# The count of the remaining experts, loaded into all engines' registers two blocks before the end of the work instead of after it

## The chip, the cores and the metric

One core of a Trainium2 chip. The metric is the device time of one execution in microseconds (us); the kernel before was timed three times. The engines are named as in the profile: PE (matmuls) and PEld (its weight loads), DVE, ACT, POOL and SP; a "q" behind a name (PEldq, SPq) marks what the engine's sequencer does by itself: waits for semaphores, register loads, branches.

## What is computed

Three layers follow each other. The change lies in the last one, a mixture of experts in which each token takes one expert, and may keep that of the token before it:

```python
def _moe2_ref(x, w_gate, w_local, w1, w2) -> np.ndarray:
    ...
    for b in range(B):
        prev_e = -1
        for s in range(S):
            fresh_e = int(np.argmax(logits[b, s]))
            if s == 0 or local_gate[b, s] < 0.5:
                e = fresh_e
            else:
                e = prev_e if prev_e >= 0 else fresh_e
            prev_e = e
            ...
            h = np.maximum(x[b, s] @ w1[e], 0.0)
            out[b, s] = p[e] * (h @ w2[e])
```

There are 4 batch rows of 576 tokens, a width of 512, 8 experts and 1024 hidden units an expert. Ahead of it stand a linear attention (4 x 8 heads) and a mixing and feed-forward layer (512 to 2048 to 512).

## The kernel before

Activations lie transposed in `y`, features on partitions and tokens along the row. Each float32 product is made of three matmuls: weights and activations are split into a high part and a rest (`hi`, `lo`, `hhi`, `hlo`, `w[:, 0]`, `w[:, 1]`), and high times high, high times rest and rest times high are summed in PSUM.

The instruction order is that in which the Python code issues them (`manual_schedule`); each engine runs its own instructions in that order, and semaphores hold it where it needs another engine's result. The feed-forward layer and the experts are worked through in `blocks`, `n` of them. A block is one group of weights (a unit: four pieces for the first matrix, four for the second) against a stretch of 384 or 288 tokens. For each batch row `b` the kernel first finds out, on the chip, which expert most tokens use (`route(b)`), and runs this one expert for all 576 tokens: two units of weights (`g` 0 and 1), each against two stretches (`c` 0 and 1) of 288 tokens. So the last block, `n - 1`, is row 3, g 1, c 1, and `n - 2` is row 3, g 1, c 0.

`mm1(i, f)` is the first matrix of block `i`, hidden rows `f` (12 matmuls), followed by ACT's ReLU into `hhi` (L511) and DVE's rest `hlo` (L512). `mm2(i, d)` is the second matrix (12 matmuls), and for g 1 it is followed by DVE's addition into `y` (L534), a product with the tokens' probabilities (L537; POOL's, but DVE's for the last two pieces of the last block), and the store of the piece (L548). `work()` orders them: while block `i` is worked on, the ReLU pieces of block `i + 1` are made ahead, so an iteration `i` issues `mm1(i+1, 0)`, then `mm2(i, 0..3)`, then `mm1(i+1, 1..3)`. Between these pieces `side(i, step)` issues what runs beside them, among it `w_prep`, which splits the next piece of weights: a cast on ACT (L168) and a subtraction on DVE (L172).

Tokens may use other experts than the one that was run. `route` writes into `flags`, 32 numbers on one partition, a one for each other (row, expert) that is in use. Behind the last block DVE sums them (L815), casts the sum to an integer (L816), and `values_load` (L817) has each of the five engines load it into a register (TENSOR_LOAD). A loop (L819) then runs once per such expert. In this execution no pass of the loop was run: each engine tests its register, branches past the loop's code, and meets the others in the closing barrier.

Of the kernel before, what the change touches and what calls it, by code (L numbers as in the profile page):

```python
# [7 lines left out]
F32 = mybir.dt.float32  # L8
F32R = mybir.dt.float32r
U32 = mybir.dt.uint32  # L10
I32 = mybir.dt.int32
ACTF = mybir.ActivationFunctionType
ALU = mybir.AluOpType
AX = mybir.AxisListType.X
# [22 lines left out]
def model(ctx, tc, kq, vx, wphi, ident, up, vp, wff, wg, wmoe, rconst, outT):  # L37
    nc = tc.nc
# [137 lines left out]
    late = {}  # L176
# [24 lines left out]
    def w_ahead():  # L201

        if at["dma"] < len(pieces) and at["dma"] < at["prep"] + 2 and (
                pieces[at["dma"]][0].kind == "ffn" or pieces[at["dma"]][0].b in pidx):
            w_dma()
# [261 lines left out]
    ul = {0: later}  # L467
# [29 lines left out]
    def mm1(i, f):  # L497
        u, hf, t0, n_, _ = blocks[i]
        w = need(u, f)
        hi, lo = ul[hf]  # L500
        sl = slice(t0, t0 + n_)
        ps = fps()[:, :n_]
        for k in range(4):
            wh = w[:, 0, k * 128:(k + 1) * 128]
            wl = w[:, 1, k * 128:(k + 1) * 128]
            nc.tensor.matmul(ps, lhsT=wh, rhs=hi[:, k, sl], start=(k == 0), stop=False)  # L506
            nc.tensor.matmul(ps, lhsT=wh, rhs=lo[:, k, sl], start=False, stop=False)  # L507
            nc.tensor.matmul(ps, lhsT=wl, rhs=hi[:, k, sl], start=False, stop=(k == 3))  # L508
        hhi = h_p.tile([128, CF], F32R, tag="hhi", name="hhi")[:, :n_]
        hlo = h_p.tile([128, CF], F32R, tag="hlo", name="hlo")[:, :n_]  # L510
        nc.scalar.activation(out=hhi, in_=ps, func=ACTF.Relu)  # L511
        nc.vector.scalar_tensor_tensor(out=hlo, in0=ps, scalar=0.0, in1=f32(hhi), op0=ALU.max, op1=ALU.subtract)  # L512
        hh[i, f] = (hhi, hlo)
        if last[u] == i:
            used.add((units.index(u), f))

    def mm2(i, d):
        u, hf, t0, n_, c = blocks[i]
        ps = fps()[:, :n_]
        for f in range(4):  # L520
            hhi, hlo = hh[i, f]
            w = need(u, 4 + f)
            wh = w[:, 0, d * 128:(d + 1) * 128]
            wl = w[:, 1, d * 128:(d + 1) * 128]
            nc.tensor.matmul(ps, lhsT=wh, rhs=hhi, start=(f == 0), stop=False)  # L525
            nc.tensor.matmul(ps, lhsT=wl, rhs=hhi, start=False, stop=False)  # L526
            nc.tensor.matmul(ps, lhsT=wh, rhs=hlo, start=False, stop=(f == 3))  # L527
        if last[u] == i and d == 3:
            used.update((units.index(u), 4 + f) for f in range(4))
        dst = y[:, hf, d, t0:t0 + n_]  # L530
        if u.kind == "moe" and u.g == 0:
            nc.scalar.copy(out=dst, in_=ps)
            return
        nc.vector.tensor_tensor(out=dst, in0=ps, in1=dst, op=ALU.add)  # L534
        if u.kind == "moe":
            eng = nc.vector if i + 1 == n and d > 1 else nc.gpsimd
            eng.tensor_tensor(out=dst, in0=dst, in1=scale[u.b][:, c * CH:(c + 1) * CH], op=ALU.mult)  # L537
            outs.append((outT[d * 128:(d + 1) * 128, 2 * S * hf + t0:2 * S * hf + t0 + n_], dst))
            if i + 1 == n:
                store(0)  # L540
# [3 lines left out]
    def store(keep):  # L544
        while len(outs) > keep:
            dst, src = outs.pop(0)
            eng = nc.scalar if keep else nc.sync
            eng.dma_start(out=dst, in_=src)  # L548
# [138 lines left out]
    def drain(lst):  # L687
        while lst:
            if next(lst[0], "end") == "end":
                lst.pop(0)  # L690


    n = len(blocks)
    splits = []

    def side(i, step):

        u, _, _, _, c = blocks[i]
        if u.kind == "ffn":
            if splits and step in (2, 6):  # L700
                split_rows(*splits.pop(0))
            if u.g < 3:
                for _ in range(2 if step in (3, 7) else 1):
                    if not preps and room() and at["prep"] < min(8 * u.g + 16, 8 * u.g + 10 + 4 * c // 3 if u.g else 16):
                        preps.append(w_prep())
                    prep_step()
                if late:
                    w_ahead()
            else:
                if step == 0 and c in (2, 3, 5):  # L710
                    bg.append(route({2: 0, 3: 1, 5: 2}[c]))
                bg_step()
                if 0 not in pidx:
                    bg_step()
                if 0 in pidx and step % 2:
                    if at["prep"] < 8 * len(ffn_units) + 8 and room():
                        preps.append(w_prep())
                        drain(preps)
                        w_ahead()
        else:  # L720
            k = units.index(u)
            if u.b == 0 and u.g == 0 and c == 0 and step == 0:
                bg.append(route(3))
            bg_step()
            if c == 0 and step == 4 and u.g == 0:
                bg.insert(0, scale_row(u.b))
            if k + 1 < len(units) and at["prep"] < min(8 * (k + 2), 8 * k + 8 + 4 * c + (step + 1) // 2) and room():
                v = units[k + 1]
                if v.b not in pidx:
                    drain(bg)  # L730
                preps.append(w_prep())
                drain(preps)
                w_ahead()

    def work():

        for f in range(4):
            mm1(0, f)
            yield
        for i in range(n):  # L740
            u = blocks[i][0]
            if u.kind == "moe" and u.g == 1 and u.b not in scale:
                drain(bg)
            if i + 1 < n:
                mm1(i + 1, 0)
            side(i, 0)
            yield
            for d in range(4):
                mm2(i, d)
                side(i, 1 + d)  # L750
                yield
            if i + 1 < n:
                for f in range(1, 4):
                    mm1(i + 1, f)
                    if f > 1:
                        store(1)
                    side(i, 4 + f)
                    yield

    todo = work()  # L760
    ahead = [0]

# [27 lines left out]
    ul_p = late["ul"] = ctx.enter_context(tc.tile_pool(name="ulb", bufs=1))  # L790
# [4 lines left out]
    flags = late["flags"] = ul_p.tile([1, 32], F32, name="flags")  # L795
# [14 lines left out]

    left = ul_p.tile([1, 1], F32, name="left")
    lefti = ul_p.tile([1, 1], I32, name="lefti")
    nc.vector.tensor_reduce(out=left, in_=flags, axis=AX, op=ALU.add)  # L815
    nc.vector.tensor_copy(out=lefti, in_=left)  # L816
    nl = nc.values_load(lefti[0:1, 0:1], min_val=0, max_val=28)  # L817
    l_p = ctx.enter_context(tc.tile_pool(name="lp", bufs=1))
    with tc.For_i(0, nl):  # L819
        f8 = l_p.tile([1, 8], F32, name="l_f8")  # L820
# [142 lines left out]
```

## Time and profile before

| | us |
|---|---|
| median of 3 runs (lowest, highest) | 826.02 (825.59, 826.67) |
| the profiled execution's own time | 825.34 |
| its span, from the first to the last instruction | 823.5 |
| PE busy | 798.1 (97%) |
| DVE, ACT, POOL busy | 476.7 (58%), 268.6 (33%), 175.9 (21%) |

The span is what the rows are read from; the profiled execution took 1.8 us more than it. Times in rows are counted from the start of the span. Busy time counts no register loads, branches and waits for semaphores, so that an engine without busy time can still be what holds the end.

### The profile page before, as it was taken

How to read it: one execution, taken by the hardware profiler on the slowest of the kernel's cores; microseconds unless marked ns; L12 is line 12 of the kernel's file. 1: busy time of each engine (PE TensorE's matmuls, PEld its weight loads, DVE VectorE, ACT ScalarE, POOL GpSimd, SP SyncE). 2: the span in 40 equal slices, each digit the busy share in tenths (PEclk: the TensorE clock that was granted, in tenths of full speed). 3: DMA queues.
4: the chain of work that ended last, by engine and by line, in shares of the span. 5: the costliest groups of instructions: out<-in, count | busy, mean ns of one | idle time of the engine just before them, and what ended most of it. 6: DMA issues, size and time to landing. Idle time of an engine off the chain costs nothing.

```text
span 823.5 us, 18728 instructions
## 1 busy us (share of the span) xinstructions
PE 798.1 (97%) x7904; PEld 769.5 (93%) x7904; DVE 476.7 (58%) x951; ACT 268.6 (33%) x602; POOL 175.9 (21%) x203
## 2 busy tenths in 40 slices
PE   7899999999999999999999999999999999999995
PEld 5788889999989999999999999989999999999995
DVE  5888797652588454464544532266755857435332
ACT  4666767652321111111111211112243333333330
POOL 0212323200354212132212310202030512202101
PEclk9999999999999999999999999999999999999998
DMA  5443334110022101020100100002112332423311
GB/s 176 146 137 117 126 113 138 48 44 2 2 77 77 52 26 52 27 72 32 52 27 30 48 1 1 1 2 79 52 41 65 92 102 81 145 79 108 117 39 68
DMA packets 24679, 55.39 MB, mean 67 GB/s; under 512 B 3152, under 2 KB 8016, under 8 KB 24592
## 3 DMA queue, kind: packets, MB, share of 16 engines
q1 hardware_dynamic: 20448, 50.02, 18.9%
q10 hardware_dynamic: 3888, 3.98, 1.4%
q8 instruction: 64, 1.05, 0.5%
q0 software_dynamic: 256, 0.15, 0.1%
q14 instruction: 23, 0.19, 0.1%
HBM read 49.28 MB, written 4.72 MB: 66 GB/s over the span
## 4 chain that ended last, share of the span: by engine, by line
PE 81%; DVE 10%; ACT 3%; POOL 2%; issue 1%; DMA 1%; SPq 0%; DVEq 0%; ACTq 0%
PE psf L506 11%; PE psf L525 11%; PE psf L527 11%; PE psf L526 11%; PE psf L508 11%; PE psf L507 11%; PE kv L315 3%; PE num L349 2%; PE pj L280 2%; DVE pg L285 2%; PE tq L329 1%; DVE mx L283 1%; POOL cv_w L71 1%; DVE cv_w L84 1%; PE glps L567 1%
## 5 line engine op out<-in xcount | busy, mean ns | idle before, releaser
L527 PE MATMUL psf<-hlo,w 128*128 128x384 f32 (+1 forms) x640 | 204.4, 319 | 2.2 <-DVE hlo L512 2.2
L525 PE MATMUL psf<-hhi,w 128*128 128x384 f32 (+1 forms) x640 | 205.2, 321 | 0.2 <-ACT hhi L511 0.2
L526 PE MATMUL psf<-hhi,w 128*128 128x384 f32 (+1 forms) x640 | 203.8, 319 | 0.0
L512 DVE SCALAR_TENSOR_TENSOR hlo<-psf,hhi 128x384 fp32r<-128x384 f32 (+1 forms) x160 | 82.3, 516 | 165.2 <-ACT hhi L511 164.7
L511 ACT ACTIVATE hhi<-psf 128x384 fp32r<-128x384 f32 (+1 forms) x160 | 73.2, 459 | 263.2 <-PE psf L508 259.0
L527 PEld LDWEIGHTS psf<-hlo,w 128*128 128x128 f32 x640 | 120.1, 188 | 3.4 <-DVE hlo L512 3.3
L525 PEld LDWEIGHTS psf<-hhi,w 128*128 128x128 f32 x640 | 120.1, 188 | 1.1 <-ACT hhi L511 0.5
L526 PEld LDWEIGHTS psf<-hhi,w 128*128 128x128 f32 x640 | 120.2, 188 | 0.0
L534 DVE TENSOR_TENSOR y<-psf,y 128x384 f32<-128x384 f32 (+1 forms) x128 | 67.3, 528 | 79.5 <-PE psf L527 79.2
L506 PE MATMUL psf<-hi_a,w 128*128 128x384 f32 (+1 forms) x320 | 103.3, 323 | 0.0
L506 PE MATMUL psf<-hi_b,w 128*128 128x384 f32 (+1 forms) x320 | 103.1, 322 | 0.0
L508 PE MATMUL psf<-hi_a,w 128*128 128x384 f32 (+1 forms) x320 | 102.3, 320 | 0.0
L507 PE MATMUL psf<-lo_a,w 128*128 128x384 f32 (+1 forms) x320 | 102.3, 320 | 0.0
L508 PE MATMUL psf<-hi_b,w 128*128 128x384 f32 (+1 forms) x320 | 102.3, 320 | 0.0
L507 PE MATMUL psf<-lo_b,w 128*128 128x384 f32 (+1 forms) x320 | 102.3, 320 | 0.0
L71 POOL TENSOR_TENSOR cv_w<-cv_w,cv_b 128x256 f32<-128x256 f32 x64 | 46.0, 740 | 225.9 <-DVE cv_b L87 204.2
L172 DVE TENSOR_TENSOR w<-raw,w 128x512 fp32r<-128x512 f32 x64 | 52.1, 814 | 30.8 <-ACT w L168 30.2
L168 ACT CAST w<-cv_w 128x512 fp32r<-128x512 f32 x32 | 19.9, 621 | 131.6 <-POOL cv_w L71 131.4
L506 PEld LDWEIGHTS psf<-hi_a,w 128*128 128x128 f32 x320 | 60.1, 188 | 1.0 <-issue 0.3
L506 PEld LDWEIGHTS psf<-hi_b,w 128*128 128x128 f32 x320 | 60.1, 188 | 1.0 <-issue 0.3
L508 PEld LDWEIGHTS psf<-hi_b,w 128*128 128x128 f32 x320 | 60.1, 188 | 0.0
L508 PEld LDWEIGHTS psf<-hi_a,w 128*128 128x128 f32 x320 | 60.1, 188 | 0.0
(135 smaller groups left out, 1171.2 us busy)
## 6 DMA issues: line engine op xcount, KB each, us to landing
raw<-in_wff SPq DMA_DIRECT2D x32, 512.0 KB, 3.5
raw<-in_wmoe SPq DMA_DIRECT2D x64, 256.0 KB, 2.6
kq<-in_kq SPq DMA_DIRECT2D x15, 576.0 KB, 3.8
vt<-in_vx SPq DMA_DIRECT2D x16, 325.0 KB, 3.0
outT<-y ACTq DMA_DIRECT2D x27, 144.0 KB, 3.0
outT<-y SPq DMA_DIRECT2D x5, 144.0 KB, 1.8
kq<-in_kq SPq DMA_DIRECT2D x3, 192.0 KB, 3.0
rawc<-in_vp SPq DMA_DIRECT2D x2, 288.0 KB, 4.0
```

The costliest lines, as they stand in the source:

```text
L71: eng.tensor_tensor(out=dst[:, sl], in0=a[:, sl], in1=b[:, sl], op=op)
L172: nc.vector.tensor_tensor(out=w[:, 1], in0=f, in1=f32(w[:, 0]), op=ALU.subtract)
L315: nc.tensor.matmul(out[c], lhsT=e[:, half, i, c], rhs=rhs, start=(tl == 0 and half == 0), stop=(tl == 8 and half == 1), skip_group_check=True)
L506: nc.tensor.matmul(ps, lhsT=wh, rhs=hi[:, k, sl], start=(k == 0), stop=False)
L507: nc.tensor.matmul(ps, lhsT=wh, rhs=lo[:, k, sl], start=False, stop=False)
L508: nc.tensor.matmul(ps, lhsT=wl, rhs=hi[:, k, sl], start=False, stop=(k == 3))
L511: nc.scalar.activation(out=hhi, in_=ps, func=ACTF.Relu)
L512: nc.vector.scalar_tensor_tensor(out=hlo, in0=ps, scalar=0.0, in1=f32(hhi), op0=ALU.max, op1=ALU.subtract)
L525: nc.tensor.matmul(ps, lhsT=wh, rhs=hhi, start=(f == 0), stop=False)
L526: nc.tensor.matmul(ps, lhsT=wl, rhs=hhi, start=False, stop=False)
L527: nc.tensor.matmul(ps, lhsT=wh, rhs=hlo, start=False, stop=(f == 3))
L534: nc.vector.tensor_tensor(out=dst, in0=ps, in1=dst, op=ALU.add)
```

## The change

The tiles `left` and `lefti`, the sum, the cast and the register load move from behind the last block into a function `count()`, which `work()` calls at the head of iteration `n - 2`, before it issues `mm1(n-1, 0)`. The loop behind the work takes the register values from there. Nothing else changes; lines behind the new function move down.

```diff
+    def count():
+
+        left = late["ul"].tile([1, 1], F32, name="left")
+        lefti = late["ul"].tile([1, 1], I32, name="lefti")
+        nc.vector.tensor_reduce(out=left, in_=late["flags"], axis=AX, op=ALU.add)
+        nc.vector.tensor_copy(out=lefti, in_=left)
+        late["nl"] = nc.values_load(lefti[0:1, 0:1], min_val=0, max_val=28)
+
     def work():
...
         for i in range(n):
             u = blocks[i][0]
+            if i == n - 2:
+                count()
             if u.kind == "moe" and u.g == 1 and u.b not in scale:
                 drain(bg)
             if i + 1 < n:
...
-    left = ul_p.tile([1, 1], F32, name="left")
-    lefti = ul_p.tile([1, 1], I32, name="lefti")
-    nc.vector.tensor_reduce(out=left, in_=flags, axis=AX, op=ALU.add)
-    nc.vector.tensor_copy(out=lefti, in_=left)
-    nl = nc.values_load(lefti[0:1, 0:1], min_val=0, max_val=28)
+    nl = late["nl"]
     l_p = ctx.enter_context(tc.tile_pool(name="lp", bufs=1))
     with tc.For_i(0, nl):
```

On PE this puts the register load between the last matmuls of `mm1(n-2, 3)` and the first of `mm1(n-1, 0)`, with the semaphores that the load waits for (DVE_49 is DVE's count of finished instructions):

```order
 L507 MATMUL psf<-lo_b,w 128x288
 L508 MATMUL psf<-hi_b,w 128x288
+L741 TENSOR_LOAD lefti [waits DMAHW2_49,DMAHW3_49,DMAHW1_49,DMAHW4_49,DMAHW0_49,DMAHW5_49,DVE_49,DMAHW6_49,PE_49,DMAHW7_49,Activation_49,Pool_49]
 L506 MATMUL psf<-hi_b,w 128x288 [waits Activation_49]
 L507 MATMUL psf<-lo_b,w 128x288
```

Of the semaphores named, the counts waited for on the DMA queues, PE, ACT and POOL are the same as in the kernel before and were reached long before; that on DVE is the cast's.

On DVE the sum and the cast now stand behind the last `hlo` of block `n - 2` and the last piece of weights of the kernel (L172), and the rows at the end of the work are gone:

```order
 L512 SCALAR_TENSOR_TENSOR hlo<-psf,hhi 128x288 x2
 L172 TENSOR_TENSOR w<-raw,w 128x512
+L739 TENSOR_REDUCE left<-flags 1x1
+L740 CAST lefti<-left 1x1
+L741 TENSOR_LOAD lefti
 L512 SCALAR_TENSOR_TENSOR hlo<-psf,hhi 128x288
 L534 TENSOR_TENSOR y<-psf,y 128x288 x4
```

On SP, which issues the loads of weights and the last five stores, the load moves from behind the stores to behind the last piece of weights:

```order
 L149 DMA raw<-in_wmoe 128x512
+L741 TENSOR_LOAD lefti
+L741 ISA x2
 L548 DMA outT<-y 128x288 x5
-L817 TENSOR_LOAD lefti
-L817 ISA x2
```

On ACT and POOL the load moves to the same place of the program: on ACT behind the cast of the last piece of weights (L168), on POOL behind the products of block `n - 3`.

## Rows read from the trace of the kernel before

**Rows 1.** The page: span and busy time.
```profile
span 823.5 us, 18728 instructions
PE 798.1 (97%) x7904; PEld 769.5 (93%) x7904; DVE 476.7 (58%) x951; ACT 268.6 (33%) x602; POOL 175.9 (21%) x203
```

**Rows 2.** Chain that ended last, 795 to 823.5 us: shares by line, last pieces (start, us).
```profile
by line: PE psf L527 15.3%; PE psf L526 14.8%; PE psf L525 14.8%; PE psf L507 8.4%; PE psf L506 8.4%; PE psf L508 8.4%; DVE y L534 1.6%; DVE y L537 1.6%; DVE lefti L816 0.5%; DVE left L815 0.3%; issue 0.2%
...
815.39 0.46 DVE y L537
815.97 0.14 DVE lefti L816
```

**Rows 3.** Windows: length, PE busy (later column 1.00: its granted clock), from `mm1(n-1, 0)` to the last matmul.
```profile
795.50:814.90 19.40, 19.36 (x146) 19.02 (x144) 6.63 (x15) 2.56 (x6) 4.84 (x6) 1.00 0.16 54
```

**Rows 4.** Timeline (start, us, engine, line) around the new place of the count.
```profile
795.39 0.29 PE L508 MATMUL psf<-hi_b,w 128*128 128x288 f32 x1
...
795.51 0.29 PE L506 MATMUL psf<-hi_b,w 128*128 128x288 f32 x1
...
795.71 0.41 ACT L511 ACTIVATE hhi<-psf 128x288 fp32r<-128x288 f32 x1 [1.17 <-PE psf L508]
...
796.16 0.46 DVE L512 SCALAR_TENSOR_TENSOR hlo<-psf,hhi 128x288 fp32r<-128x288 f32 x1 [1.12 <-ACT hhi L511]
...
796.66 0.69 DVE L172 TENSOR_TENSOR w<-raw,w 128x512 fp32r<-128x512 f32 x1
```

**Rows 5.** Tile lefti: duration ns min/median/max, first and last start.
```profile
L817 SPq TENSOR_LOAD <-lefti x1: 281/281/281, 816.3 to 816.3; - x1
...
L817 PEldq TENSOR_LOAD <-lefti x1: 769/769/769, 816.4 to 816.4; - x1
```

**Rows 6.** Line 958, the kernel's end: register move before the loop, closing barrier.
```profile
L958 POOLq EVENT_SEMAPHORE  x4: 17/17/17, 822.7 to 823.4; - x4
...
L958 SPq DRAIN  x3: 7/7/13, 821.7 to 822.9; - x3
...
L958 PEldq DRAIN  x2: 8/8/8, 822.7 to 823.0; - x2
...
L958 PEldq MOVE  x1: 34/34/34, 817.3 to 817.3; - x1
```

**Rows 7.** Timeline around PE's longest wait for DVE, 247 us.
```profile
246.78 0.55 DVE L512 SCALAR_TENSOR_TENSOR hlo<-psf,hhi 128x384 fp32r<-128x384 f32 x1
...
247.38 0.44 PE L527 MATMUL psf<-hlo,w 128*128 128x384 f32 x1 [1.47 <-DVE hlo L512]
247.67 0.34 PE L525 MATMUL psf<-hhi,w 128*128 128x384 f32 x1
247.84 0.34 PE L526 MATMUL psf<-hhi,w 128*128 128x384 f32 x1
```

**Rows 8.** Line 817, what PE's sequencer waited for ahead of its load.
```profile
L817 PEldq EVENT_SEMAPHORE  x6: 51/51/3486, 812.3 to 816.3; - x6
```

**Rows 9.** Line 819, the loop's test and exit, on ACT; on PE from 817.75 us.
```profile
L819 ACTq COMPARE_BRANCH  x3: 38/38/58, 817.1 to 818.4; - x3
...
L819 PEldq COMPARE_BRANCH  x1: 3332/3332/3332, 817.7 to 817.7; - x1
```

**Rows 10.** Line 819 on SP, 817.6 to 818.25 us, then 820.7 to 823.
```profile
L819 SPq EVENT_SEMAPHORE  x8: 17/17/17, 817.7 to 818.2; - x8
...
L819 SPq EVENT_SEMAPHORE  x12: 28/28/28, 820.7 to 821.4; - x12
```

**Rows 11.** Line 819 on PE, 821 to 823 us.
```profile
L819 PEldq EVENT_SEMAPHORE  x12: 51/51/51, 821.1 to 822.3; - x12
```

**Rows 12.** Line 548 on SP, the last five stores.
```profile
L548 SPq DMA_DIRECT2D outT<-y x5: 332/333/353, 805.0 to 815.9; - x5
...
DMA to landing us min/median/max: 1.8/1.8/1.8
```

**Rows 13.** Windows, 819 to 820 us; 0.51 is PE's granted clock.
```profile
819.00:820.00 1.00, 0.00 (x0) 0.00 (x0) 0.00 (x0) 0.00 (x0) 0.00 (x0) 0.51 0.03 8
```

## The prediction

> **What bounds the kernel now.** The page comes first: PE is busy for 798.1 of 823.5 us [rows 1]. Then the chain that ended last, over the two final blocks: it runs through PE's matmuls alone, then through DVE's last addition and product, the sum (L815) and the cast (L816), and it stops at 816.11 us, although the span ends at 823.5 [rows 1, 2]. So two things matter: PE up to its last matmul, and the 7.4 us behind 816.11 in which no engine is counted as busy. For PE I read the windows: from 795.50 to 814.90 us it is busy for 19.36 of 19.40 us, at the full granted clock [rows 3]. Whatever holds PE in this stretch moves the end by its full length; there is no slack that could swallow it. For the quiet end I read the rows of single lines, which list sequencers' work too: the register loads [rows 5], the loop's test and exit [rows 9 to 11], the barrier [rows 6].
>
> **What the change adds: a wait on PE.** Each engine runs in order. PE's load stands ahead of `mm1(n-1, 0)`, and it waits until DVE's cast is done. DVE's cast stands behind DVE's work on the block that PE has just finished. So PE has to stand still until ACT and DVE have caught up. Step by step, in times of the kernel before:
>
> 1. The last matmul of `mm1(n-2, 3)` starts at 795.39 and takes 0.29, and the next one, the first of `mm1(n-1, 0)`, starts at 795.51 [rows 4]. The load comes between these two.
> 2. ACT's `hhi` runs from 795.71 to 796.12, DVE's `hlo` from 796.16 to 796.62, and DVE's L172, behind ACT's cast of the last weights, from 796.66 to 797.35 [rows 4]. None of these waits for a matmul of `mm1(n-1, 0)`, so their times stay.
> 3. Sum and cast: at the end of the kernel the product on DVE ended at 815.39 + 0.46 = 815.85 [rows 2], and the cast behind it at 815.97 + 0.14 = 816.11 [rows 2]. That is 0.26 for both; the cast would end at 797.61.
> 4. PE's load began at 816.4, took 0.769 [rows 5], and the next instruction of PE's sequencer came at 817.3 [rows 6]: 1.19 after the cast's end, which gives 798.80.
> 5. Restart of the array: after the one long wait for DVE, `hlo` ended at 246.78 + 0.55 = 247.33 and the matmul started at 247.38, 0.05 later; the one behind it came 0.29 after, where the next step is 0.17 [rows 7]. The first weights have nothing to hide behind, which costs 0.12. First matmul 798.85, and 0.12 lost behind it.
>
> The stall is 798.85 - 795.51 + 0.12 = **3.46 us**. Nothing else hides it: the matmuls that stood there before are just those held.
>
> Bounds. No register load on PE with matmuls behind it is in this trace; there is only the one at the end. At the lower end PE would not wait for the answer and go on as soon as the load is issued: 0.77 + 0.1 less, 2.6 us. I take the full time, since the sequencer's next instruction came after the load's end though it is only a register move [rows 5, 6]. At the upper end: PE's sequencer stood at line 817 from 812.3 on, while its matmuls ran up to 814.9; it is some 2.5 us ahead of the array [rows 3, 8], and after the stall this lead is gone. If some ten of the waits that PE's sequencer meets in the last two blocks then show with 0.05 each, the length of one such instruction [rows 11], that is 0.5 more: 4.0. I take none of it.
>
> The Trainium skill, "DMA: Bandwidth & Descriptors", section "Latency and other measured facts", gives a `tensor_load` a floor of about 600 ns. By it the stall would be some 0.17 shorter, an estimate from that page of 3.3 us. The rows differ from it both ways (769 ns on PE, 281 ns on SP), and the rows decide.
>
> The loads on the other engines are covered. SP takes 0.28, and its next work, the stores, begins at 805.0 [rows 5, 12]. ACT and DVE have nothing until `mm1(n-1, 0)` is done, and that is late itself by 3.4 us. POOL waits for a product of `mm2(n-2)`, later still.
>
> **What the change removes: the load at the end.** It looks like the 1.19 us of the load and the 0.26 of sum and cast ahead of it. But what ends last behind it? PE leaves the loop by a branch that takes 3.33 us [rows 9], goes through 12 waits from 821.1 to 822.3 [rows 11], and reaches the barrier at 822.7. POOL, which collects the engines, goes on at the same 822.7, and 0.8 us later the span ends [rows 6]. SP reaches the barrier at 821.7: its last store is issued at 815.9 and lands 1.8 us later [rows 12], it goes on at 817.7, branches at 818.2, and its next instruction comes at 820.7 [rows 10], 2.5 us behind. The load is not in SP's way, because SP waits for the landing of the store, and that hangs on DVE's product. Without the load PE can branch at about 814.9 + 0.4 = 815.3 (the 0.4 from the move at 817.3 [rows 6] to the long branch at 817.7 [rows 9]), is out at 818.6, and 1.6 later, as now from 821.1 to 822.7, in the barrier at 820.2. Then SP at 821.7 ends last. The gain is 822.7 - 821.7; the sums of the durations around put it at 0.9 to 1.0, and I take **0.95 us**. Bounds: nothing, if SP's exit becomes as long as PE's (3.33 for 2.5); 822.7 - 820.2 = 2.5, if SP's exit shrinks until PE ends last again.
>
> The Trainium skill, "Runtime: NRT & Kernel Launch", section "Instruction fetch mechanics", says that a taken branch to code outside what has been prefetched has to fetch it before the engine goes on. The rows fit this: PE and SP, whose loop bodies are long, pay 3.3 and 2.5 us, and ACT at most 0.06. It speaks against the change, since SP's fetch remains whatever is done about the load; by the rule the gain is the 0.95, and without it 2.5.
>
> **Sum.** 3.46 - 0.95 = +2.5 us. On the profiled execution 825.34 + 2.5 = 827.8. This execution lies 0.68 under the median of the runs, so on the median 826.02 + 2.5 = **828.5 us**, 0.3% slower. About 0.2%, 1.65 us, is what a measurement of this kernel can tell from no change.
>
> **Rivals.**
>
> *The early count costs nothing* (not slower). It would if DVE had the cast done before PE's sequencer came to the load. PE's sequencer is there ahead of the array, and DVE's sum stands behind L172, which ends 1.7 us after PE's last matmul before the load [rows 4]. It would need PE to pass the load. Then only the end counts: -0.95, or up to -2.5 with the upper bound of the gain, 825.1 to 823.5. The stall has to fall under 0.95 for it to decide. 4%, half of it beyond 0.2%.
>
> *PE does not wait for its load's answer.* The stall is 2.6, the sum +1.6, 827.6, within 0.2%. For it speaks only that no such row exists. 4%.
>
> *SP's exit gets shorter*, since PE's fetch no longer runs beside it. Both fall in the same few microseconds now, PE's from 817.7 and SP's from 818.2. From 0.85 us less on, the sum falls under 1.65; at the bound it is +0.95, 827.0. Against it: SP's own 2.5 is already shorter than PE's. 6%.
>
> *The clock falls during the stall.* PE would be idle from 795.68 to 798.85, 3.2 us. At the end of the kernel the granted clock, full until PE's last matmul [rows 3], averages 0.51 from 819 to 820 us, half (1.2 for 2.4 GHz) for nearly all of it [rows 13]: it fell at about 819, some 4.1 us behind the last matmul. The idle time here is shorter than that. If it falls, each microsecond at half clock costs half of one; were it back after as long as it took to fall, that is 2.05 more, 830.6 (at most it is the rest of PE's work, 19.4 us). 6%.
>
> **How the numbers follow.** The forecast, a stall of 2.9 to 4.0 and a gain of 0 to 1.6, has 80%. Slower by over 0.2% holds it and the clock's case, 86%. Within 0.2% lie the load without a wait, SP's shorter exit and half of the free count, 12%; faster, 2%. The bounds together give +0.1 to +4.0; with single terms at their ends +1.6 to +3.5. The runs of before spread by 0.4 to 0.65 around the median. From +1.0 to +4.0 holds eight in ten or a little more: 827.0 to 830.0.
>
> **What would show it.** In the trace of the changed kernel: PE's one new gap of about 3.2 us ahead of `mm1(n-1, 0)`, ended by its load and not by a matmul's operand, and DVE's sum right behind L172 (steps 1 to 3); PE's load of 0.7 to 0.8 (step 4); PE busy without gaps from there to its last matmul; sum and cast absent at the end, PE in the barrier before SP, and SP's exit branch again followed by 2.5 us. From DVE's last product to the end of the span it should be 6.7 us, where it is 7.65 now. The prediction is wrong if the gap is under 2 us, if matmuls run behind the load before its end, if the granted clock falls before the last matmul, or if the end shrinks by more than 1.6 us.

## The result, and the profile after

The changed kernel took 829.99 us in the median of 6 runs (829.28 to 832.24), the kernel before 825.81 (824.97 to 826.76, 6 runs, three of them the ones reported above). The ratio is 1.0054, with an interval of 1.0039 to 1.0070: 4.5 us slower, 3.2 to 5.8. The direction is the predicted one; the size is nearly twice the 2.5 us forecast, and over the +4.0 at which the range ended. The profiled execution took 830.23 us, with a span of 828.5, 5.0 more than before. PE reached the place of the change 0.7 us later than in the profile before ([rows 4]: 795.39 for the last matmul of `mm1(n-2, 3)`; here 796.13). Runs of one kernel differ by that much ahead of this place (the three profiles of the changed kernel below come to it between 794.83 and 796.13), so the rest, 4.3 us, is the change.

The timeline around the new place (start, us, engine, line; in brackets the idle time before), which answers to [rows 4]:

```profile
796.13 0.29 PE L508 MATMUL psf<-hi_b,w 128*128 128x288 f32 x1
796.46 0.41 ACT L511 ACTIVATE hhi<-psf 128x288 fp32r<-128x288 f32 x1 [1.17 <-PE psf L508]
...
796.90 0.46 DVE L512 SCALAR_TENSOR_TENSOR hlo<-psf,hhi 128x288 fp32r<-128x288 f32 x1 [1.12 <-ACT hhi L511]
797.41 0.69 DVE L172 TENSOR_TENSOR w<-raw,w 128x512 fp32r<-128x512 f32 x1
798.01 0.17 DVE L739 TENSOR_REDUCE left<-flags 1x1 f32<-1x32 f32 x1
798.22 0.14 DVE L740 CAST lefti<-left 1x1 int32<-1x1 f32 x1
...
799.21 0.37 PE L506 MATMUL psf<-hi_b,w 128*128 128x288 f32 x1 [2.79 <-issue]
...
799.55 0.29 PE L508 MATMUL psf<-hi_b,w 128*128 128x288 f32 x1
```

`hhi`, `hlo`, L172, sum and cast follow each other as in the prediction's steps 1 to 3, and PE stands idle for 2.79 us behind them. The row names "issue" as the cause, since no operand was missing; what PE's sequencer did is in the rows of the load (duration ns min/median/max, first and last start), which answer to [rows 5, 8]:

```profile
L741 PEldq EVENT_SEMAPHORE  x6: 51/51/4167, 793.9 to 798.6; - x6
L741 PEldq TENSOR_LOAD <-lefti x1: 484/484/484, 798.7 to 798.7; - x1
```

One of the waits took 4.2 us; it is the one in which DVE's count stands, and it ended at 798.40, where the cast ended at 798.36. The load behind the waits took 0.484, where 0.769 had been taken. Counted at the third matmul (799.55 - 796.13 = 3.42 after the one ahead of the gap, where three undisturbed steps of 0.13 take 0.39), the stall is 3.03 us.

Then the windows (length, busy times, and as the third number from the end PE's granted clock), which answer to [rows 3]:

```profile
801.00:803.00 2.00, 2.00 (x10) 2.00 (x9) 0.46 (x1) 0.41 (x1) 0.00 (x0) 0.50 0.00 0
...
804.50:820.00 15.50, 15.50 (x118) 15.33 (x116) 4.74 (x11) 1.23 (x3) 4.84 (x6) 1.00 0.20 68
```

Behind the gap PE's granted clock is half, 1.2 GHz: 10 matmuls lie in 2 us, where the filled kernel (e2, below) has 17 at full clock. PE is not waiting here; it counts as busy, so only the clock's column shows the loss. Windows around it put the change to half at about 800.6 and back at 804.0.

Last the end, with the rows of SP's stores, of SP's exit in two stretches, and of the barrier, which answer to [rows 6, 10, 12]:

```profile
L548 SPq DMA_DIRECT2D outT<-y x4: 332/333/348, 816.9 to 821.2; - x4
...
DMA to landing us min/median/max: 1.8/1.8/2.3
```

```profile
L825 SPq EVENT_SEMAPHORE  x8: 17/17/17, 823.5 to 824.0; - x8
...
L825 SPq EVENT_SEMAPHORE  x12: 28/28/28, 826.7 to 827.4; - x12
```

```profile
L964 POOLq EVENT_SEMAPHORE  x4: 17/17/17, 827.7 to 828.4; - x4
...
L964 SPq DRAIN  x3: 7/7/13, 827.6 to 827.9; - x3
...
L964 PEldq DRAIN  x2: 8/8/8, 825.3 to 828.0; - x2
```

As forecast, PE is in the barrier before SP (825.3 and 827.6), and SP is the last. But the last store landed 2.3 us after its issue (821.2 to 823.5), not 1.8, and that moved all of SP's exit. DVE's last product ended at 820.69 + 0.46 = 821.15, 7.3 us before the end of the span; before it was 7.65. The end gave 0.3 back instead of 0.95.

```profile
820.69 0.46 DVE L537 TENSOR_TENSOR y<-y,sbc 128x288 f32<-128x288 f32 x1
```

### The profile page after: what moved, and what is told of

Its sections match the earlier page's. It is cut to its first block, busy times and chain, and to the rows that moved or that the text cites. A ratio compares the mean times of both kernels' runs of the same rounds, so it can differ in the third digit from the quotient of the medians.

```text
span 828.5 us, 18728 instructions
## 1 busy us (share of the span) xinstructions
PE 800.8 (97%) x7904; PEld 772.2 (93%) x7904; DVE 477.2 (58%) x951; ACT 268.6 (32%) x602; POOL 175.9 (21%) x203
## 5 line engine op out<-in xcount | busy, mean ns | idle before, releaser
L172 DVE TENSOR_TENSOR w<-raw,w 128x512 fp32r<-128x512 f32 x64 | 52.3, 816 | 30.5 <-ACT w L168 29.9
L168 ACT CAST w<-cv_w 128x512 fp32r<-128x512 f32 x32 | 19.9, 621 | 131.5 <-POOL cv_w L71 131.3
L506 PEld LDWEIGHTS psf<-hi_a,w 128*128 128x128 f32 x320 | 60.1, 188 | 1.0 <-issue 0.3
L507 PEld LDWEIGHTS psf<-lo_b,w 128*128 128x128 f32 x320 | 60.2, 188 | 0.0
```

Of the source, the lines that this page charges most:

```text
L168: nc.scalar.copy(out=w[:, 0], in_=f)
L172: nc.vector.tensor_tensor(out=w[:, 1], in0=f, in1=f32(w[:, 0]), op=ALU.subtract)
```

## The experiments

The theory after this result: the loss is a stall of 3.0 us on PE, plus some 1.5 to 1.7 us by the clock's fall behind it, less what the end gives back. The rivals: the clock has no part in it (a matter of that one run); the load costs by itself wherever it stands; sum and cast on DVE delay PE. Differences are ratios to the kernel before, timed beside each kernel on the same chip, with their intervals.

**Sum and cast earlier (e1), and half of the change (e3).** e1 splits `count()`: sum and cast at `n - 3`, the load where the change put it. e3 keeps sum and cast at the change's place and puts the load back behind the last block. (The lines that split `count()` into `count()` and `load()` are left out.)

```diff
-            if i == n - 2:
+            if i == n - 3:
                 count()
+            if i == n - 2:
+                load()
```

```diff
+    load()
     nl = late["nl"]
```

> Sum and cast one block earlier than in the changed kernel, the register load in its place. If the loss is PE's wait for DVE's sum, PE's gap ahead of mm1(n-1, 0) goes (under 0.3 us), the granted clock stays full there, and only the end counts: 0.3 to 1.0 us faster than the kernel before. If the load on PE costs by itself, wherever its value is ready, a gap of 0.5 us or more stays and the time is at or over that of the kernel before.

> Half of the change: sum and cast at the new place, the register load behind the last block as before. If only the load's wait on PE costs, no gap, full clock, and sum and cast (0.26 us) are off the end: 0 to 0.3 us faster than the kernel before. If sum and cast on DVE delay PE by themselves, 0.3 us or more slower.

e1: 0.9996 (0.9986 to 1.0005); e3: 0.9995 (0.9986 to 1.0005). Neither can be told from the kernel before, and so the runs do not tell e1's expected gain of 0.3 to 1.0 us from none. In e1 PE's load stands at the changed kernel's place, and PE does not stop there (the load, then the windows, columns as above):

```profile
L744 PEldq TENSOR_LOAD <-lefti x1: 486/486/486, 795.4 to 795.4; - x1
...
793.00:816.00 23.00, 23.00 (x176) 22.89 (x175) 8.25 (x17) 3.90 (x9) 4.84 (x6) 1.00 0.17 57
```

So the load is free where its value is ready, and sum and cast are free where nobody waits for them. Only the two together, at one place, cost. Both keep PE's early exit, and yet gain little: their last stores landed after 2.3 and 2.6 us.

**One piece later (e4).** The count stands behind `mm1(n-1, 0)`, with one `hlo` and no piece of weights ahead of the sum.

```diff
                 mm1(i + 1, 0)
             side(i, 0)
+            if i == n - 2:
+                count()
             yield
```

> The whole count one piece later, behind mm1(n-1, 0) and what stands beside it, so that DVE has only one hlo ahead of the sum and no piece of weights. If the stall is the work that stands ahead of the sum on ACT and DVE, it shrinks by that piece (0.7 us), from 3.0 to about 2.3, and the time is 1.3 to 2.0 us over the kernel before with a full clock, 3.0 to 3.7 if the clock falls here too. If the stall is a fixed price of the load on PE, it stays at 3.0 and the time at that of the changed kernel.

The profile shows a gap of 2.05 us and the third matmul 2.29 us late (the one ahead of the gap starts at 796.76), and in this run the clock stayed full behind it:

```profile
799.10 0.37 PE L525 MATMUL psf<-hhi,w 128*128 128x288 f32 x1 [2.05 <-issue]
...
799.44 0.29 PE L527 MATMUL psf<-hlo,w 128*128 128x288 f32 x1
```

The stall follows the work ahead of the sum, as the theory has it. The time was 1.0041 (1.0028 to 1.0054), 3.4 us. The eight runs fall into two groups, three from 827.1 to 828.1 and five from 829.2 to 830.2. Their medians lie 2.2 us apart. A clock that falls in some runs would give two groups, some 1.5 us apart; the one profile is of the fastest run, without a fall, so that this is not shown.

**The gap filled (e2, e11), beside the changed kernel again (e12).** 21 matmuls whose result nothing uses stand ahead of PE's load.

```diff
             if i == n - 2:
+                fill = late["psr"].tile([128, CH], F32, tag="r1", bufs=2, name="fill")
+                for _ in range(21):
+                    nc.tensor.matmul(fill, lhsT=u.w[0][:, 0, 0:128], rhs=ul[1][0][:, 0, S:S + CH], start=True, stop=True)
                 count()
```

> The changed kernel with 21 matmuls of 128x288 put ahead of PE's load, whose result nothing uses; they take 21 x 0.133 = 2.8 us, about as long as the gap. If the clock's fall is a part of the loss of its own, the delay of mm1(n-1, 0) stays at about 3 us, the clock stays full, and the time is 2.0 to 2.8 us over the kernel before, some 1.7 less than the changed kernel. If the clock is not part of it (the loss is all in the stall and the end), 4 to 4.5 us over the kernel before, as the changed kernel.

> The changed kernel with 21 matmuls in PE's gap once more, beside the changed kernel itself on the same chip, since the first timing (2.9 us over the kernel before in the medians) lay between the two theories. If the clock's fall is a loss of its own of 1.7 us, this kernel is 1.0 to 2.0 us under the changed one, with the clock full from the gap to the last matmul. If not, the two are within 0.5 us.

> The changed kernel, beside the filled one: 4.0 to 4.8 us over the kernel before, with the clock at half for 3.4 us behind the gap.

e2 took 1.0038 (1.0024 to 1.0052), 2.9 us in the medians, just above the range that the clock's theory had given, so it was run again with the changed kernel on the same chip: the filled kernel 828.35 (827.87 to 828.94, 5 runs), the changed one 829.49 (829.40 to 830.91, 5 runs), with ratios of 1.0037 (1.0023 to 1.0050) and 1.0053 (1.0039 to 1.0067). Every run of the one lies under every run of the other; the medians differ by 1.1 us, within the 1.0 to 2.0 expected. In the profile of e2 the last matmul of `mm1(n-2, 3)` starts at 794.99, so that the third behind the load, at 798.41, is late by the same 3.03 us; the clock stays full:

```profile
796.83 1.21 PE L753 MATMUL fill<-hi_b,w 128*128 128x288 f32 x8
...
798.41 0.30 PE L508 MATMUL psf<-hi_b,w 128*128 128x288 f32 x1
```

```profile
801.00:803.00 2.00, 2.00 (x17) 2.00 (x16) 0.46 (x1) 0.00 (x0) 0.80 (x1) 1.00 0.03 8
```

From the third matmul behind the gap to the last of the kernel there is the same work in both. Here are the last ones, first of e2, then of the changed kernel:

```profile
817.20 0.29 PE L527 MATMUL psf<-hlo,w 128*128 128x288 f32 x1
```

```profile
819.87 0.29 PE L527 MATMUL psf<-hlo,w 128*128 128x288 f32 x1
```

e2 needs 817.20 - 798.41 = 18.79 us, the changed kernel 819.87 - 799.55 = 20.32. The kernel before needs 814.57 - 795.78 = 18.79 for it. The clock's fall cost 1.53 us.

**Twice (e5), and the changed kernel itself (e7).** e5 makes the count a second time, four blocks earlier.

```diff
-            if i == n - 2:
+            if i in (n - 6, n - 2):
                 count()
```

> The changed kernel with the whole count made a second time, at the same place of the batch row before (four blocks earlier, behind the same work on DVE). If each such wait costs a stall of 3.0 us and, where PE's idle time of 2.8 us makes the granted clock fall, 1.7 us behind it, the time is 7.5 to 9.0 us over the kernel before, twice the changed kernel's loss, with two gaps of 2.8 us and two stretches at half clock in the profile. If the clock's fall in the changed kernel was a matter of that run or of the place in the kernel, one stretch or none, and 5.5 to 6.5 us over.

> The changed kernel itself once more, beside the kernel before on the same chip. If the clock's fall behind the gap of 2.8 us is the rule, the mean granted clock is lower than that of the kernel before by 0.002 in most of the runs (1.7 of 828 us), and the time is 4.0 to 4.8 us over. If it falls in few runs, 2.5 to 3.2 us over in the median.

e7: 1.0042 (1.0028 to 1.0056), 3.4 us, between the two ranges; the three timings of the changed kernel gave 4.5, 3.4 and 4.4 (e12). The mean granted clock of e7's runs was 0.9936, that of the kernel before beside it 0.9948. The difference is short of 0.002, so it does not settle in how many runs the clock fell. In the profile of e7 the clock fell behind the gap of 2.79 us again, as it did in the profile of e12 behind 2.82: three of three profiles of the changed kernel. e5: 1.0065 (1.0046 to 1.0084), 5.4 us, just under both ranges. One of its six runs took 834.85 us, at a mean clock of 0.991 where the others have 0.995; no profile shows what it met. The two gaps in the profile of another:

```profile
745.23 0.37 PE L506 MATMUL psf<-hi_b,w 128*128 128x288 f32 x1 [2.25 <-issue]
```

```profile
800.32 0.37 PE L506 MATMUL psf<-hi_b,w 128*128 128x288 f32 x1 [2.52 <-DVE lefti L740]
```

```profile
745.00:755.00 10.00, 9.77 (x74) 9.80 (x75) 3.48 (x7) 1.54 (x3) 3.92 (x4) 1.00 0.28 76
800.00:820.00 20.00, 19.43 (x144) 19.12 (x144) 5.70 (x13) 1.64 (x4) 4.83 (x6) 1.00 0.15 52
```

Both are shorter than 2.79, and the clock stayed full behind both. The second load's gap is shorter since it waits for DVE alone; the first one's list of other semaphores has been met. The first gap is shorter since PE loads nothing there. The loop reads the registers of the second count alone, and at the first place only SP has a load; PE and the others stop for the semaphores and go on (tile lefti):

```profile
L741 SPq TENSOR_LOAD <-lefti x2: 276/282/288, 744.9 to 799.8; - x2
...
L741 PEldq TENSOR_LOAD <-lefti x1: 486/486/486, 799.8 to 799.8; - x1
```

So 2.25 us are what the wait for the cast and the list of semaphores cost without a load, and the load adds about its own 0.5 to make the changed kernel's 2.79. Counted at the third matmul, PE was 2.49 us late at the first place and 2.76 at the second, 5.25 together, near the 5.4 of the runs. The wait came twice, and the clock's part did not come. As both gaps are shorter than those of the changed kernel, e5 does not say whether the place in the kernel has a part in the fall.

**PE's exit held back (e6, e9, e8), beside e1 again (e10).** In all kernels with an early exit of PE the last store landed late. Behind PE's exit branch a block of instructions of 16 KB is fetched by a DMA (in the changed kernel the branch starts at 820.35, the block at 821.31), and this now meets the store. e6 is e1 with 18 unused matmuls (2.4 us) behind the last block, so that PE's branch comes as late as before; e8 has 9 (1.2 us).

```diff
     drain(bg)
+    fill = late["psr"].tile([128, CH], F32, tag="r1", bufs=2, name="fill")
+    for _ in range(9):
+        nc.tensor.matmul(fill, lhsT=ul[1][0][:, 0, 0:128], rhs=ul[1][0][:, 0, S:S + CH], start=True, stop=True)
     right.close()
```

> The kernel with sum and cast one block earlier and the load two blocks before the end, with 18 more matmuls of 128x288 (2.4 us) behind the last block, whose result nothing uses, so that PE takes its exit branch, and fetches code, 2.4 us later, as late as in the kernel before. If PE's fetch beside the last store is what makes that store land 2.3 to 2.7 us after its issue instead of 1.8, it lands 1.8 after here, SP is in the barrier some 5.9 us after DVE's last product (6.6 with the early branch), PE comes in last again, and the time is that of the kernel before within 0.4 us. If the later landing has another cause, it stays at 2.3 or more.

> The kernel with 18 such matmuls (PE's branch 2.4 us later) once more. Its profile says that PE ends last, 6.8 us after DVE's last product, as in the kernel before, so by the trace the time is that of the kernel before within 0.4 us. If the 1.1 us under the kernel before of its first timing hold, the trace lacks something that I have not seen.

> Sum and cast one block earlier, load two blocks before the end, and 9 matmuls of 128x288 (1.2 us) behind the last block, whose result nothing uses: PE's exit branch comes some 0.6 us after DVE's last product, late enough that its fetch begins when the last store's packets have left, and early enough for PE to be in the barrier before SP. If the last store's landing and SP's exit are all that is left of the end, the store lands 1.8 after its issue, SP is in the barrier last, 5.9 us after DVE's last product, and the time is 0.7 to 1.2 us under the kernel before: the gain at the end that the prediction reckoned with. If PE's fetch still meets the store, the landing is over 2.0 and the gain 0.5 or less.

> Sum and cast one block earlier, load two blocks before the end, no matmuls behind the last block, once more and beside the two others: 0 to 0.5 us under the kernel before, with the last store landing at 2.3 or more and 7.3 to 7.5 us from DVE's last product to the end.

e6 gave 0.9986 (0.9976 to 0.9996), faster than its profile could explain; timed again (e9), the same kernel gave 0.9996 (0.9986 to 1.0006), so I take the first for scatter. e8 gave **0.9981 (0.9972 to 0.9991)**, 1.6 us faster than the kernel before, more than the 0.7 to 1.2 expected, and the best of all; e10, the same without the matmuls, 0.9990 (0.9979 to 1.0001), 0.8 us faster where 0 to 0.5 were expected. On this same chip and in this same series e8's median is 1.2 us under that of e9 and 0.6 under that of e10. The last store landed 1.8 us after its issue in e6, e8 and e9, and 2.3 to 2.9 after in the ten profiles with an early exit. The DMA queues of the changed kernel from 821.3 to 822.3 us, and then of e8 while its last store moves (queue, kind: packets, MB, share of 16 engines):

```profile
q1 hardware_dynamic: 76, 0.09, 25.2%
q8 instruction: 1, 0.02, 5.8%
```

```profile
q1 hardware_dynamic: 144, 0.15, 58.8%
```

In the changed kernel a block of instructions (q8) is under way while the store's packets (q1) come; in e8 all 144 packets of the store pass alone, and the block follows. The single packets show the tie: in all ten profiles with an early exit the last packet of the store ended 0.75 us behind the end of the block, whether the block took 0.93 us (changed kernel: 822.24, then 822.99) or 1.45 (e12: 821.51, then 822.26); in the four others the store's packets were through before the block began. The barrier of e8:

```profile
L972 SPq DRAIN  x3: 7/7/13, 822.0 to 822.3; - x3
L972 PEldq DRAIN  x2: 8/8/8, 821.4 to 822.3; - x2
```

PE comes in at 821.4, SP at 822.0. DVE's last product ended at 815.86, so the end takes 7.0 us up to the span's 822.8, 0.66 less than before. In the profiles of e9 and e10 it takes 7.9 and 7.7, so that the ends give e8 an advantage of 0.9 and 0.7, near the 1.2 and 0.6 of the medians. Against the kernel before, 0.66 is near the lower end of e8's interval (0.7); the rest of the 1.6 is not explained by its profile, and e6 and e9 show that two timings of one kernel can differ by 0.8.

## Why the prediction was wrong

What failed is one rival's chance and one term, and they add up; a stall that was shorter than forecast took a part of it back.

- **The clock.** "The clock falls during the stall" had 6% and stood in the sum as nothing, with the argument that at the end of the kernel the clock fell only 4.1 us behind the last matmul [rows 13]. That row says when the clock fell once PE had stopped for good; it does not say how short a rest can bring a fall. In the three profiles of the changed kernel the clock fell after PE had been idle for 2.8 us, and it fell 1.1 to 1.4 us after PE had started again. The loss was 1.53 us (the rival's price was 2.05). e2 and e11, with the gap filled, show that this part goes when PE is kept busy, while the stall stays.
- **The end.** "0.95" was 0.3 in the first profile of the changed kernel and nothing in the two others (0.1 and 0.2 lost): the landing of the last store, taken as 1.8 [rows 12], became 2.3 to 2.9. The prediction had PE's fetch move ahead and asked only whether SP's exit would get shorter by that; it did not ask what the fetch would meet at its new time. In e8, where the two are kept apart, the landing is 1.8 again and the end gives 0.66 back; the other 0.29 went into SP's exit, 2.77 us behind its branch for 2.48 in the kernel before.
- **The stall.** 3.46 was forecast, 3.03 measured. Steps 1 to 3 hold to a few hundredths. Step 4 was off: PE's load took 0.484 for 0.769, and the first matmul came 0.85 after the cast's end for 1.24. Step 5's loss behind the restart was 0.07 for 0.12. The upper bound by the lost lead of PE's sequencer did not show: PE was busy without a gap behind the stall.

By the profile: 3.03 + 1.53 - 0.3 = 4.3; forecast 3.46 - 0.95 = 2.5. The stall was 0.4 under the forecast, the clock added 1.5, and the end gave 0.65 less. The mechanism, a load that makes PE wait for DVE's sum, was right, and e1, e3 and e4 show it; "not slower", "no wait for the answer" and a shorter exit of SP are out. One sum of the prediction is off without weight in the forecast: with single terms at their ends the lowest value is 3.46 - 2.5 = +1.0, not +1.6.

Open is when a gap brings the clock's fall. In the 14 profiles of nine kernels, waits of 1.9 us and, in most, 0.7 near 30 us went with half clock in 12, and one of 1.5 us at 247 us in one (e10); gaps of 2.05, 2.25 and 2.52 us were not followed by it, those of 2.79 to 2.82 were. Length alone does not order these. The fall near 30 us also sets executions of one kernel apart: the profile of the kernel before is one of the two without it, that of the changed kernel has it (granted clock from 32 to 36 us, first of the kernel before; from 32.7 to 35.9 of the changed one).

```profile
32.00:36.00 4.00, 3.29 (x103) 2.98 (x102) 3.53 (x9) 3.61 (x10) 2.81 (x2) 1.00 0.01 3
```

```profile
32.70:35.90 3.20, 3.20 (x60) 3.08 (x62) 2.52 (x8) 2.35 (x7) 1.76 (x2) 0.50 0.01 3
```

## What to carry to other kernels

A value that is loaded into all engines' registers stops each engine that comes to the load before the value is there, the bottleneck engine too; make the value well ahead and load it later (e1), and the load is free. Price a stall on PE together with the clock: a stop may cost half as much again behind it, where PE counts as busy (here 1.5 us behind stops of 2.8, and nothing behind those of 2.05 to 2.5 in the profiles). And ask of work that gets earlier what it meets there: here a fetch of code ran into the last store and took back most of the gain at the end.

## What the runs showed of the hardware that was not expected

- PE's granted clock went to half (1.2 GHz) for 3.4 us after idle times of as little as 1.5 us (in one profile of 14). In the changed kernel it fell 1.1 to 1.4 us after PE had started again; in e10 it fell at 248.58, within the gap, which ended at 248.80.
- The same register load took 769 ns on PE in the kernel before and 484 to 489 ns in the changed kernel, e1 and e3, on ACT 662 and about 470. In the kernel before, the last store was being moved at that time; whether that is the cause was not tried.
- A store beside a fetch of 16 KB of instructions landed after 2.3 to 2.9 us, alone after 1.8. Nine more matmuls without use, 1.2 us of PE, hold the fetch back, and with them the kernel was faster than without in the medians (824.66 for 825.26; the intervals against the kernel before overlap).
